# Weights into spaces that stand idle: three gate/up blocks of the last group, and one down block of two groups

## The chip, the cores and the metric

The kernel runs on one core of a Trainium2 chip. The metric is the time of one execution on the device in microseconds (us). A profile of one execution stands beside it, whose span is the time from the first to the last instruction of the program.

The engines are TensorE (PE, matmuls), VectorE (DVE), ScalarE (ACT), GpSimd (POOL) and SyncE (SP). In this kernel SP and POOL mostly ask for transfers between HBM and the on-chip memory: SP for the inputs, the gate/up weights, the outputs and the transposes, POOL for the down weights and for the attention values. Each of them issues its requests in program order, and a request that has to wait (for a buffer to be free, or for data) holds up all that is behind it.

## What is computed

A transformer block over 2048 rows of 576 numbers, in bfloat16, conditioned by a vector `c` (a shift, a scale and a gate for each of its two halves):

```python
mod = (silu(c) @ w_mod).reshape(c.shape[0], 6, 1, -1)
sa, ca, ga, sb, cb, gb = ...
h = layernorm(x) * (1 + ca) + sa
x = x + ga * attention(h)          # 32 heads of 18, each row sees 8 rows: itself and -2, -4, ... -14
h = layernorm(x) * (1 + cb) + sb
g = h @ w_gate                     # 576 x 4608
u = h @ w_up                       # 576 x 4608
x = x + gb * ((g * u) @ w_down)    # 4608 x 576
```

## The kernel before

The rows are cut into 8 chunks of 256, and the chunks into 5 groups: [0], [1, 2], [3, 4], [5, 6], [7]. For each group a gate/up phase makes hh = g * u, transposed (4608 rows as 36 f-tiles of 128), and a down phase multiplies hh by w_down and adds up over the f-tiles. All five groups read all weights again from HBM. While TensorE works on one group, attention and layernorm of the next chunks run beside it on VectorE, ScalarE and in gaps that a planner (`timed`, `among`) leaves for TensorE's share of them. The planner knows costs of the engines' work; requests for weights have no cost in it, they are put at fixed f-tiles.

**Blocks.** Weights come in blocks of 4 f-tiles, so a phase has 9 blocks (`NBLK`), numbered in the code from 0 to 8. A gate/up block is 1 MB, asked for by `load_wgu` (line 154, two requests on SP, gate and up, of 512 KB each). A down block is 576 KB, asked for by `load_wd` (line 171, one request on POOL). A block number g counts over groups, g = group x 9 + block, and numbers over 8 reach into the next group.

**Buffers.** Gate/up blocks rotate through 3 buffers (`wgup`), down blocks through 3 others (`wdp`). A block can instead be given a home of its own: `wgu_home` and `wd_home` hold a space for a block number, and the loader takes it if there is one. Before the change, the homes are these: the product space `prod_t` (the products of queries and keys, 5120 columns) takes down blocks 3 and 4 in groups 1 to 3 (5 and 6 in group 0); in groups 0 and 4, which have one chunk only, the second half of the hh tile is spare and takes some blocks, in group 4 the down blocks 3 to 6 (`ld_spare`), which wait for the landing of the last gate/up block.

**Gate/up** (`gate_up`, matmuls at line 694 in `half`). For each f-tile, gate and up matmuls run as a pair on two halves of the array. At every fourth f-tile, a block two ahead is asked for: at f = 4 block 3, at f = 8 block 4, and so on to block 8 at f = 24 (group 0 has a list of its own). A buffer is free for it when the block three before it has been read out.

**Down** (`down`, lines 895 and 900, `acc` and the narrow rest `accr`). Blocks 0 to 2 are there at the start, blocks 3 and 4 in the product space. Block 5, 6 and 7 are asked for after blocks 0, 1 and 2, block 8 after block 5, and then the first three of the next group after blocks 6 and 7 and at the end of the phase. In the middle, three gate/up blocks of the next group are asked for (f = 1, 15 and 25). The last group has a down phase of its own, `down_last` (lines 948 and 951).

**Value buffers.** Attention reads shifted copies of the values, 4608 columns per 128 rows, from two buffers in turn (`vshp`, tile `vsh`, requests at line 440 on POOL, arithmetic at lines 499 to 509, the last of which writes `o_sb`). `o_sb` is then transposed by a request on SP (line 582, to `oT`), and TensorE multiplies it by the output weights (`b_w`, lines 588 and 590) at a place that the planner sets in the down phase. After that come a layernorm, another transpose on SP (line 620, to `h2T`) and the scale and shift, before the group's gate/up can begin.

Of the kernel before, what the change touches and what calls it, by code (L numbers as in the profile page):

```python
# [7 lines left out]
BF = mybir.dt.bfloat16  # L8
# [10 lines left out]
P = 128  # L19
D = 576  # L20
# [3 lines left out]
H = 32  # L24
DH = 18
W = 8
# [9 lines left out]
NB = 512  # L36
FB = 4
# [7 lines left out]
def kernel(  # L45
# [20 lines left out]
    def pool(name, bufs, **kw):  # L66
        return ctx.enter_context(tc.tile_pool(name=name, bufs=bufs, **kw))
# [14 lines left out]
    vshp = pool("vshp", 2)  # L82
# [33 lines left out]
    prod_t = consts.tile([P, 4 * KT * CH], BF, name="prod_t")  # L116
# [25 lines left out]
    wgu_blk, wgu_in, wd_blk, wd_home, wgu_home = {}, {}, {}, {}, {}  # L142
    NG = len(GROUPS)
    NBLK = FT // FB

    def load_wgu(g):
        if g >= NG * NBLK:
            return
        cs = slice((g % NBLK) * NB, (g % NBLK + 1) * NB)
        wb = wgu_home.pop(g, None)  # L150
        if wb is None:
            wb = wgup.tile([P, KF, 2, NB], BF, name="wgu")
        for t, wsrc in enumerate((B_w_gate, B_w_up)):
            r = nc.sync.dma_start(wb[:, :, t, :], wsrc[0:KF * P, cs].rearrange("(k p) n -> p k n", p=P))
        wgu_blk[g] = wb
        wgu_in[g] = r
# [6 lines left out]
    def load_wd(g):  # L163
        if g >= NG * NBLK:
            return
        r0 = (g % NBLK) * FB * P
        wb = wd_home.pop(g, None)
        if wb is None:
            wb = wdp.tile([P, FB, D], BF, name="wd")
        wd_blk[g] = wb  # L170
        return nc.gpsimd.dma_start(wb[:], B_w_down[r0:r0 + FB * P, :].rearrange("(k p) n -> p k n", p=P))  # L171
# [624 lines left out]
    def timed(items, extra, threads, slack, busy=0.0):  # L796

        t, dve = 0.0, busy
        done, seq = {f"v{i}": 0.0 for g in GROUPS for i in g[1:]}, []
        done["late"] = 0.0  # L800
        extra, threads = list(extra), [list(th) for th in threads]

        def ready(need):
            return all(done.get(x, 1e9) <= t for x in need.split())

        def fill():
            nonlocal t, dve
            moved = True
            while moved:
                moved = False  # L810
                for th in threads:
                    if th and ready(th[0][2]) and (not th[0][1] or dve <= t + slack):
                        pe, d, _, mark, wait, call = th.pop(0)
                        t += pe
                        dve = max(dve, t) + d if d else dve
                        done[mark] = (dve if d else t) + wait
                        seq.append(("piece", call))
                        moved = True
                        break
        for kind, f, step, own, need in items:  # L820
            if seq and extra and ready(extra[0][1]):
                pe, _, mark, make = extra.pop(0)
                seq.append(("pair", make))
                t += pe
                done[mark] = t + pe + 1.0
                fill()
            assert ready(need), (need, t)
            seq.append((kind, f))
            fill()
            dve = max(dve, t) + own  # L830
            t += step
        assert not extra, (extra[0][1], t)
        return seq, [(*p[0:2], p[2] if all(x in names(th) for x in p[2].split()) else "late", *p[3:]) for th in threads for p in th]
# [22 lines left out]
    def gate_up(gi, hh, bg):  # L856
        n = len(GROUPS[gi])
        first = 2.6 if gi == 0 else 2.0 * len(GROUPS[gi - 1])
        seq, late = timed(gate_items(gi), *bg, 0.9 * n, first)
        prev = after = None  # L860
        for kind, x in seq:
            if kind == "piece":
                x()
                continue
            if after:
                after()
            cur = x() if kind == "pair" else wg_pair(gi, hh, x, kind)
            cur.first()
            after = prev.second() if prev else None
            if kind in ("f", "f1"):  # L870
                f = x
                if f > 0 and f % FB == 0:
                    ask = {1: 4, 2: 5, 3: 6, 5: 7, 6: 8}.get(f // FB, NBLK) if gi == 0 else f // FB + 2
                    if ask < NBLK:
                        load_wgu(gi * NBLK + ask)
                loads.get((gi, f), nop)()
            prev = cur
        if after:
            after()
        after = prev.second()  # L880
        if after:
            after()
        return late

    def down(gi, hh, bg):
        grp = GROUPS[gi]
        nj = ST * len(grp)
        last = FT - FB
        at, late = among(last, 0.25 * nj, bg)
        acc = [ps([P, 512], F32, "acc") for _ in range(nj)]  # L890
        accr = ps([P, 2 * ST, 64], F32, "accr")

        def mm_a(f, j):
            wb = wd_blk[gi * NBLK + f // FB]
            nc.tensor.matmul(acc[j][:], lhsT=hh[:, f, js(j)], rhs=wb[:, f % FB, 0:512],  # L895
                             start=(f == 0), stop=(f == FT - 1))

        def mm_r(f, j):
            wb = wd_blk[gi * NBLK + f // FB]
            nc.tensor.matmul(accr[:, j, :], lhsT=hh[:, f, js(j)], rhs=wb[:, f % FB, 512:D],  # L900
                             start=(f == 0 and j == 0), stop=(f == FT - 1), skip_group_check=True)

        for f in range(last):
            for j in range(nj):
                mm_a(f, j)
                mm_r(f, j)
            if f % FB == FB - 1:
                ask = {0: 7, 1: 8, 2: 9, 7: 10} if gi == 0 else {0: 5, 1: 6, 2: 7, 5: 8, 6: 9, 7: 10}
                if f // FB in ask:
                    load_wd(gi * NBLK + ask[f // FB])  # L910
            asks = (1, 5 * FB, 6 * FB + 2) if gi == 0 else (1, 4 * FB - 1, 6 * FB + 1)
            if f in asks:
                load_wgu((gi + 1) * NBLK + asks.index(f))
            for piece in at[f]:
                piece()
        xs = [t for i in grp for t in x1.pop(i)]
        for j in range(nj):
            for f in range(last, FT):
                mm_r(f, j)
        o_ts = [outp.tile([P, D], BF, name="o_t") for _ in range(nj)]  # L920
        t_r = outr.tile([P, 2 * ST, 64], BF, name="t_r")
        nc.vector.tensor_tensor(t_r[:, 0:nj, :], accr[:, 0:nj, :],
                                gb_bc[:, None, 512:D].to_broadcast([P, nj, 64]), ALU.mult)
        for j in range(nj):
            for f in range(last, FT):
                mm_a(f, j)
            nc.vector.tensor_tensor(o_ts[j][:, 0:512], acc[j][:], gb_bc[:, 0:512], ALU.mult)
        for j in range(nj):
            r0 = (grp[0] * ST + j) * P
            nc.vector.tensor_tensor(o_ts[j][:, 0:512], o_ts[j][:, 0:512], xs[j][:, 0:512], ALU.add)  # L930
            nc.vector.tensor_tensor(o_ts[j][:, 512:D], t_r[:, j, :], xs[j][:, 512:D], ALU.add)
            nc.sync.dma_start(out_flat[r0:r0 + P, :], o_ts[j][:])
        load_wd(gi * NBLK + NBLK + 2)
        return late

    def down_last(gi, hh):
# [55 lines left out]
    def behind(dma, load):  # L992
        tc.add_manual_dep(dma.ins, load.ins.name, SYNC, reason="order of the loads")
# [197 lines left out]
    def ld_spare(k):  # L1191
        g = (NG - 1) * NBLK + 3 + k
        wd_home[g] = spare[NG - 1][:, k * FB * D:(k + 1) * FB * D].rearrange("p (k d) -> p k d", d=D)
        behind(load_wd(g), wgu_in[NG * NBLK - 1])

    def ld_prods(gi):
        for k in range(2):
            g = gi * NBLK + (5 if gi == 0 else 3) + k
            wd_home[g] = prod_t[:, k * FB * D:(k + 1) * FB * D].rearrange("p (k d) -> p k d", d=D)
            load_wd(g)  # L1200

    loads = {(0, 20): lambda: behind(load_wd(1), wgu_in[6]), (0, 21): lambda: ld_d1(4), (0, 22): lambda: load_wd(2), **{(gi, 32): lambda gi=gi: ld_prods(gi) for gi in (1, 2, 3)}, (NG - 1, 28): lambda: [ld_spare(k) for k in range(4)]}

    def ld_d1(k):
        c0 = 8 * NB + FB * D if k == 3 else 0
        wd_home[k] = spare[0][:, c0:c0 + FB * D].rearrange("p (k d) -> p k d", d=D)
        load_wd(k)
# [56 lines left out]
    for gi, grp in enumerate(GROUPS):  # L1264
        hh_t = hhp.tile([P, FT * 2 * CH], BF, name="hh")
        n = CH * len(grp)
# [45 lines left out]
```

## Time and profile before

| | us |
|---|---|
| three runs | 548.65, 550.29, 550.65 |
| median | 550.29 |
| the profiled execution | 549.95 |
| its span | 548.2 |

Times in the profile are from the start of its span. Group 1's down phase runs from about 212 to 252 us, group 2's gate/up from there to 332 and its down phase to 373, group 3's gate/up to 451 and its down phase to 489, the last group's gate/up to 527 and its down phase to 543. The views used below are the page itself (a summary), the waits (who waited for whom, how long in total, how often, the longest), the timeline (instructions of an engine in order of time: start, duration, engine, line, operation, tiles written and read; behind it, in brackets, the idle time before it and what ended it), the windows (for a stretch: the mean, busy time and number of instructions of TensorE, its weight loads, VectorE, ScalarE and GpSimd, the granted clock, the DMA share and GB/s), and the view of one line, with the time from request to landing. In the queues of SP and POOL a row is the time of issuing, not of moving the data. "x2" behind a row means that two rows are shown as one.

### The profile page before, as it was taken

To read this page: it belongs to the slowest core of one execution; us is meant where nothing else is said; L and a number is where in the kernel's file an instruction comes from. 1 tells how busy PE (TensorE), PEld (TensorE's weight loads), DVE (VectorE), ACT (ScalarE), POOL (GpSimd) and SP (SyncE) were. 2 spreads that over 40 slices of the span, in tenths; PEclk is the share of its full clock that TensorE was granted. 3 is DMA by queue.
4 is the path that set the end of the run, shared out by engine and by line. 5 is a ranking of instruction groups with operands and counts; after the bars stand their busy time and mean duration, and the time that the engine had idled before them with its cause. 6 is when DMAs were issued, how large, how long until landed. Compare 5 with 4: busy or idle time off the path is not lost.

```text
span 548.2 us, 14589 instructions
## 1 busy us (share of the span) xinstructions
PE 538.7 (98%) x6190; PEld 322.5 (59%) x6190; DVE 317.6 (58%) x717; ACT 250.0 (46%) x615; POOL 70.2 (13%) x106
## 2 busy tenths in 40 slices
PE   8999999999999999999999999999999999999997
PEld 4777799756745444555544444555544445568875
DVE  5989687767866787546358896524343924031212
ACT  3666777643656564022646552103555550016630
POOL 8112111222000110112000200110020001110030
PEclk9999999999999999999999999999999999999999
DMA  8999989868873692867645972965299432758771
GB/s 285 302 299 355 306 202 315 298 183 254 299 206 88 192 287 75 206 202 236 235 110 158 260 254 69 195 205 152 92 256 291 129 90 84 228 158 273 245 234 50
DMA packets 94746, 114.52 MB, mean 209 GB/s; under 512 B 27930, under 2 KB 83370, under 8 KB 94554
## 3 DMA queue, kind: packets, MB, share of 16 engines
q1 hardware_dynamic: 83184, 67.29, 43.6%
q0 software_dynamic: 11344, 46.25, 26.8%
q8 instruction: 48, 0.79, 0.6%
q14 instruction: 16, 0.13, 0.1%
q10 hardware_dynamic: 154, 0.07, 0.0%
HBM read 103.15 MB, written 4.74 MB: 197 GB/s over the span
## 4 chain that ended last, share of the span: by engine, by line
PE 83%; DMA 7%; DVE 4%; issue 4%; ACT 1%; SPq 0%; POOL 0%; POOLq 0%; DVEq 0%; ACTq 0%
PE pg L694 25%; PE pu L694 20%; PE acc L895 16%; DMA wgu<-in_B_w_up_dram 5%; PE pq L694 3%; PE pq L401 3%; PE acc L948 3%; PE pw L590 2%; PE accr L900 2%; PE lgT L455 2%; PE pv L694 2%; DMA wd<-in_B_w_down_dram 1%; PE pv L424 1%; DVE prod_t L1033 1%; PE busy L190 1%
## 5 line engine op out<-in xcount | busy, mean ns | idle before, releaser
L694 PE MATMUL pg<-h2T,wgu 64*128 64x512 bf16 (+1 forms) x1472 | 277.7, 327 | 0.0
L694 PE MATMUL pu<-h2T,wgu 64*128 64x512 bf16 (+1 forms) x1472 | 274.1, 327 | 1.7 <-DMA wgu<-in_B_w_up_dram 1.6
L694 PEld LDWEIGHTS <-wgu 64*128 64x128 bf16 x2944 | 147.3, 94 | 98.4 <-DMA wgu<-in_B_w_up_dram 2.8
L745 ACT CAST u_sb<-pu 128x512 bf16<-128x512 f32 (+1 forms) x172 | 85.6, 497 | 142.6 <-PE pg L694 125.9
L748 DVE TENSOR_TENSOR hh<-g_sb,u_sb 128x512 bf16<-128x512 bf16 x136 | 57.4, 423 | 117.6 <-ACT g_sb L746 117.1
L895 PE MATMUL acc<-wd,hh 128*128 128x512 bf16 x376 | 93.2, 380 | 0.0
L746 ACT CAST g_sb<-pg 128x512 bf16<-128x512 f32 (+1 forms) x172 | 86.6, 504 | 0.0
L895 PEld LDWEIGHTS <-hh 128*128 128x128 bf16 x504 | 49.0, 98 | 59.6 <-issue 1.5
L900 PE MATMUL accr<-wd,hh 128*128 128x64 bf16 x376 | 63.5, 193 | 0.4 <-DMA wd<-in_B_w_down_dram 0.4
L694 PE MATMUL pu<-h2T,wgr 64*128 64x512 bf16 (+1 forms) x188 | 61.5, 327 | 0.2 <-ACT u_sb L745 0.2
L694 PE MATMUL pg<-h2T,wgr 64*128 64x512 bf16 (+1 forms) x188 | 61.5, 327 | 0.0
L171 POOL DMA_DIRECT2D wd<-in_B_w_down_dram x31 | 23.3, 751 | 227.9 <-PE pwr L588 95.6
L900 PEld LDWEIGHTS <-hh 128*128 128x128 bf16 x504 | 45.9, 98 | 2.4 <-issue 0.5
L446 DVE TENSOR_TENSOR prod_t<-qT,kT 128x1280 bf16<-128x1280 bf16 x56 | 43.7, 818 | 0.7 <-ACT kT L765 0.7
L499 DVE TENSOR_TENSOR vsh<-vsh,attn 128x1152 bf16<-128x1152 bf16 x56 | 39.6, 749 | 0.0
L694 PEld LDWEIGHTS <-wgr 64*128 64x128 bf16 x376 | 21.1, 94 | 15.4 <-issue 2.5
L895 PE MATMUL acc<-prod_t,hh 128*128 128x512 bf16 x112 | 28.9, 380 | 0.0
L440 POOL DMA_DIRECT2D vsh<-vd x14 | 12.5, 897 | 105.7 <-DVE o_sb L509 79.2
L296 ACT ACTIVATE h2T<-h2T,modc 128x256 bf16<-128x256 bf16 x12 | 6.6, 594 | 37.6 <-DMA h2T<-xn 37.6
L401 PE MATMUL pq<-hT,wqk 128*128 128x256 bf16 (+1 forms) x225 | 21.8, 251 | 0.5 <-DVE hT L294 0.5
L694 PE MATMUL pq<-hT,wqk 64*128 64x256 bf16 (+1 forms) x360 | 21.7, 259 | 0.0
L900 PE MATMUL accr<-prod_t,hh 128*128 128x64 bf16 x112 | 21.6, 193 | 0.0
(201 smaller groups left out, 565.5 us busy)
## 6 DMA issues: line engine op xcount, KB each, us to landing
wgu<-in_B_w_gate_dram SPq DMA_DIRECT2D x44, 512.0 KB, 4.6
wgu<-in_B_w_up_dram SPq DMA_DIRECT2D x44, 512.0 KB, 7.7
wd<-in_B_w_down_dram POOLq DMA_DIRECT2D x31, 576.0 KB, 4.9
vsh<-vd POOLq DMA_DIRECT2D x14, 1152.0 KB, 9.5
prod_t<-in_B_w_down_dram POOLq DMA_DIRECT2D x8, 576.0 KB, 10.3
hh<-in_B_w_down_dram POOLq DMA_DIRECT2D x6, 576.0 KB, 8.1
x_r<-in_A_x_dram SPq DMA_DIRECT2D x8, 288.0 KB, 11.8
vd<-v_sb POOLq DMA_DIRECT2D x16, 144.0 KB, 5.0
```

The costliest lines, as they stand in the source:

```text
L171: return nc.gpsimd.dma_start(wb[:], B_w_down[r0:r0 + FB * P, :].rearrange("(k p) n -> p k n", p=P))
L401: nc.tensor.matmul(pq[:, gi, :], lhsT=wqk[:, kt, m * P:(m + 1) * P], rhs=hT[:, kt, cols], start=(kt == 0), stop=(kt == KT - 1))
L440: return nc.gpsimd.dma_start(vsh[:].rearrange("p w d h -> p w (d h)"), vsrc)
L446: nc.vector.tensor_tensor(prod, aa[i]["qT"][:], aa[i]["kT"][:, :, off:off + CH], ALU.mult)
L499: nc.vector.tensor_tensor(v, v, at, ALU.mult)
L694: return nc.tensor.matmul(out, lhsT=lhs, rhs=rhs, start=first, stop=last, skip_group_check=True)
L745: nc.scalar.copy(u[:, c, :], pu)
L746: nc.scalar.copy(g[:, c, :], pg)
L748: return lambda: nc.vector.tensor_tensor(hh[:, f - c:f + 1, :], g, u, ALU.mult)
L895: nc.tensor.matmul(acc[j][:], lhsT=hh[:, f, js(j)], rhs=wb[:, f % FB, 0:512], start=(f == 0), stop=(f == FT - 1))
L900: nc.tensor.matmul(accr[:, j, :], lhsT=hh[:, f, js(j)], rhs=wb[:, f % FB, 512:D], start=(f == 0 and j == 0), stop=(f == FT - 1), skip_grou ...
L948: nc.tensor.matmul(acc[i][:], lhsT=hh[:, f, js(j)], rhs=wb(f)[:, c0:c1], start=(f == 0), stop=(f == FT - 1))
```

## The change

- In group 4 the gate/up blocks 3 and 4 (the fourth and fifth) get the two value buffers, and block 8 (the ninth) the product space. Blocks 3 and 4 are asked for in the gate/up of group 3, at f = 34. In group 4's gate/up the remaining four blocks, 5 to 8, are asked for at f = 4, 8, 12 and 16.
- In groups 1 and 2 the down block 8 gets a value buffer and is asked for together with block 6, after block 1. The first three down blocks of the next group, numbers 9 to 11, are asked for one step earlier each (after blocks 5, 6 and 7), and the request at the end of the phase goes.
- Groups 0 and 3 ask for their down blocks as before; their lists are only written in another form.

```diff
-                    ask = {1: 4, 2: 5, 3: 6, 5: 7, 6: 8}.get(f // FB, NBLK) if gi == 0 else f // FB + 2
+                    ask = {0: {1: 4, 2: 5, 3: 6, 5: 7, 6: 8}, NG - 1: {1: 5, 2: 6, 3: 7, 4: 8}}.get(gi, {k: k + 2 for k in range(NBLK)}).get(f // FB, NBLK)
                     if ask < NBLK:
                         load_wgu(gi * NBLK + ask)
                 loads.get((gi, f), nop)()
...
+    def value_space():
+        return vshp.tile([P, W, DH, H], BF, name="vsh").rearrange("p w d h -> p (w d h)")
+
+    def wgu_spaces():
+        for k, space in ((3, value_space()), (4, value_space()), (8, prod_t)):
+            wgu_home[(NG - 1) * NBLK + k] = space[:, 0:8 * NB].rearrange("p (k t n) -> p k t n", t=2, n=NB)
+        load_wgu((NG - 1) * NBLK + 3)
+        load_wgu((NG - 1) * NBLK + 4)
+
+    WD_ASKS = [{0: (7,), 1: (8,), 2: (9,), 7: (10,)},
+               {0: (5,), 1: (6, 8), 2: (7,), 5: (9,), 6: (10,), 7: (11,)},
+               {0: (5,), 1: (6, 8), 2: (7,), 5: (9,), 6: (10,), 7: (11,)},
+               {0: (5,), 1: (6,), 2: (7,), 5: (8,), 6: (9,), 7: (10,)}]
...
-                ask = {0: 7, 1: 8, 2: 9, 7: 10} if gi == 0 else {0: 5, 1: 6, 2: 7, 5: 8, 6: 9, 7: 10}
-                if f // FB in ask:
-                    load_wd(gi * NBLK + ask[f // FB])
+                if gi in (1, 2) and f // FB == 1:
+                    wd_home[gi * NBLK + 8] = value_space()[:, 0:FB * D].rearrange("p (k d) -> p k d", d=D)
+                for k in WD_ASKS[gi].get(f // FB, ()):
+                    load_wd(gi * NBLK + k)
...
-        load_wd(gi * NBLK + NBLK + 2)
+        if gi in (0, 3):
+            load_wd(gi * NBLK + NBLK + 2)
...
-    loads = {(0, 20): lambda: behind(load_wd(1), wgu_in[6]), (0, 21): lambda: ld_d1(4), (0, 22): lambda: load_wd(2), **{(gi, 32): lambda gi=gi: ld_prods(gi) for gi in (1, 2, 3)}, (NG - 1, 28): lambda: [ld_spare(k) for k in range(4)]}
+    loads = {(0, 20): lambda: behind(load_wd(1), wgu_in[6]), (0, 21): lambda: ld_d1(4), (0, 22): lambda: load_wd(2), **{(gi, 32): lambda gi=gi: ld_prods(gi) for gi in (1, 2, 3)}, (3, 34): wgu_spaces, (NG - 1, 28): lambda: [ld_spare(k) for k in range(4)]}
```

## The prediction

> **What bounds the kernel now.** First the page: its span and its line of busy times.
>
> ```profile
> span 548.2 us, 14589 instructions
> PE 538.7 (98%) x6190; PEld 322.5 (59%) x6190; DVE 317.6 (58%) x717; ACT 250.0 (46%) x615; POOL 70.2 (13%) x106
> ```
>
> TensorE is busy for 538.7 of 548.2 us, so only idle TensorE time and the start and end of the span can be won without taking matmuls away, and the change takes none away. So the next view is the list of TensorE's waits, cut to 100 to 545 us, which leaves the start-up out. Its columns are the total, the number of waits and the longest.
>
> ```profile
> engine line waited for: us in total, times, longest us
> PE pu L694 <- DMA wgu<-in_B_w_up_dram: 1.6, 2, 0.8
> PE accr L900 <- DMA wd<-in_B_w_down_dram: 0.4, 1, 0.4
> ```
>
> That is the whole list: three waits, all for weights. The timeline of TensorE shows where they are and what they really take, because the ends of matmuls are modelled and a wait is only counted from such an end. I read start to start.
>
> ```profile
> 323.53 0.38 PE L694 MATMUL pg<-h2T,wgu 64*128 64x512 bf16 x1
> 324.04 0.39 PE L694 MATMUL pu<-h2T,wgu 64*128 64x512 bf16 x1
> ...
> 368.80 0.19 PE L900 MATMUL accr<-wd,hh 128*128 128x64 bf16 x1
> 369.39 0.39 PE L900 MATMUL accr<-wd,hh 128*128 128x64 bf16 x8 [0.40 <-DMA wd<-in_B_w_down_dram]
> ...
> 490.01 0.27 PE L694 MATMUL pg<-h2T,wgr 64*128 64x256 bf16 x1
> 500.81 0.27 PE L694 MATMUL pg<-h2T,wgr 64*128 64x256 bf16 x1
> 500.92 0.27 PE L694 MATMUL pg<-h2T,wgu 64*128 64x256 bf16 x1
> 501.93 0.28 PE L694 MATMUL pu<-h2T,wgu 64*128 64x256 bf16 x1 [0.74 <-DMA wgu<-in_B_w_up_dram]
> ...
> 513.63 0.27 PE L694 MATMUL pg<-h2T,wgu 64*128 64x256 bf16 x1
> 514.74 0.28 PE L694 MATMUL pu<-h2T,wgu 64*128 64x256 bf16 x1 [0.84 <-DMA wgu<-in_B_w_up_dram]
> ```
>
> In the last group's gate/up the gate and up matmuls run as a pair and start together, so the pair at 500.92 stands for 501.93 - 500.92 = 1.01 us and the one at 513.63 for 514.74 - 513.63 = 1.11 us. The down phase of group 2 loses 369.39 - 368.80 = 0.59 us where eight such small matmuls need 0.39 us, one step of about 0.03 us: 0.56 us. A fourth gap, 0.51 us at 323.53 in group 2's gate/up, is too short to be listed as a wait; the change does not touch what feeds it.
>
> Why these three? The queue of SP shows the requests of the last gate/up.
>
> ```profile
> 494.16 0.39 SPq L154 DMA_DIRECT2D wgu<-in_B_w_gate_dram  x1
> 494.60 0.50 SPq L154 DMA_DIRECT2D wgu<-in_B_w_up_dram  x1
> 498.09 0.37 SPq L154 DMA_DIRECT2D wgu<-in_B_w_gate_dram  x1
> ...
> 506.94 0.37 SPq L154 DMA_DIRECT2D wgu<-in_B_w_gate_dram  x1
> 507.36 0.50 SPq L154 DMA_DIRECT2D wgu<-in_B_w_up_dram  x1
> ...
> DMA to landing us min/median/max: 3.9/5.4/7.3
> ```
>
> The last line is the landing time of these requests from the view of line 154 between 489 and 520 us. With three buffers, block 3 (counted from 0) is asked for only when block 0 is read out, at 494.16 us, and is needed at 500.92: 6.8 us ahead, while its up half is issued at 494.60 and lands 7.3 us later. The same for block 6: 506.94, and needed at 513.63. One f-tile takes (500.81 - 490.01) / 11 = 0.98 us here, a block of four 3.93 us, in which 1 MB must come. So it is the lead, not TensorE, that is short by about 1 us.
>
> **The change part by part.** (1) Blocks 3 and 4 of the last gate/up get the two value buffers, asked for in group 3. Are they free? The last reads of the buffers, in the timeline of VectorE, and of the product space, which block 8 takes, in TensorE's:
>
> ```profile
> 211.55 0.46 DVE L509 TENSOR_TENSOR o_sb<-vsh 128x576 bf16<-128x576 bf16 x1
> ...
> 329.94 0.46 DVE L509 TENSOR_TENSOR o_sb<-vsh 128x576 bf16<-128x576 bf16 x1
> ...
> 438.77 0.46 DVE L509 TENSOR_TENSOR o_sb<-vsh 128x576 bf16<-128x576 bf16 x1
> ...
> 473.64 0.19 PE L900 MATMUL accr<-prod_t,hh 128*128 128x64 bf16 x1
> ```
>
> They are free at 439.2 us. SP is in order: behind the transposes of the last attention output it issues blocks 3 and 4, and only then block 0, which it issues at 440.57 now.
>
> ```profile
> 440.57 0.52 SPq L154 DMA_DIRECT2D wgu<-in_B_w_gate_dram  x1
> ...
> 463.56 2.53 SPq L620 DMA_TRANSPOSE h2T<-xn  x2
> ...
> 440.00:450.00 10.00, 10.00 (x96) 4.48 (x92) 2.13 (x5) 5.64 (x11) 0.00 (x0) 1.00 0.44 121
> 450.00:460.00 10.00, 10.00 (x85) 4.94 (x82) 3.61 (x9) 2.05 (x4) 0.75 (x1) 1.00 0.21 61
> 500.00:510.00 10.00, 9.26 (x169) 8.02 (x167) 2.12 (x5) 6.03 (x19) 0.00 (x0) 1.00 0.81 251
> ```
>
> The last two columns of the windows are the DMA share and GB/s. Four more issues of about 0.5 us put block 0 at some 442.7 us; it is needed just before 490.01. The added 2.1 MB at the 251 GB/s of the last row take 8.4 us, and the DMA engines are idle for 5.6 + 7.9 = 13.5 us of those 20. SP's next work, the transposes, comes at 463.56. So the move costs nothing; without that empty stretch it would be up to 8.4 us of delay on SP's transfers.
>
> (2) In the last gate/up four blocks are asked for instead of six. Block 5 goes out when block 0 is read out, at 494.2, and is needed at f = 20, which without the stalls is 500.81 + 8 x 0.98 = 508.7 us: a lead of 14.5 us in place of 6.8. Blocks 6 and 7 follow at 498.1 and about 502.0 with the same lead; block 8 has its own space, free since 473.6, and goes out right behind block 7, needed at 520.4. 4.2 MB at 251 GB/s are 16.7 us, so the last lands near 511, ahead of its need by 9. Both stalls go: -1.01 - 1.11 = -2.12 us. The four down blocks in the spare half of hh wait for the last gate/up block, so they now start near 511 and come in before the down phase begins; TensorE waits for none of them before, so this is worth nothing.
>
> (3) The ninth down block (8) in groups 1 and 2. POOL's queue around group 2's down:
>
> ```profile
> 222.78 0.75 POOL L171 DMA_DIRECT2D wd<-in_B_w_down_dram  x1 [5.62 <-PE accr L900]
> ...
> 343.87 0.75 POOL L171 DMA_DIRECT2D wd<-in_B_w_down_dram  x1 [6.17 <-PE accr L900]
> 347.25 0.75 POOL L171 DMA_DIRECT2D wd<-in_B_w_down_dram  x1 [2.63 <-PE accr L900]
> 361.45 0.75 POOL L171 DMA_DIRECT2D wd<-in_B_w_down_dram  x1 [13.45 <-PE accr L900]
> ```
>
> Block 8 leaves at 361.45 and is used at about 368.8; now it leaves behind block 6, at 344.6, into a value buffer that has been free since 329.9 (in group 1 at 223.5, free since 211.6). No wait is added in front of block 7 at 347.25. That is -0.56 us in group 2, nothing in group 1, where TensorE did not wait. The next group's three down blocks each move one request earlier, which only empties the queue sooner. Its two value loads: one buffer is now read by TensorE until the end of the down phase, but they stood behind a request that waited for the same matmuls, so they lose nothing.
>
> The instructions are the same in number and kind on every engine; all that moves are requests. **Sum:** -2.12 - 0.56 = -2.68 us. The profiled execution took 549.95 us, so 547.27. It lies 0.34 us under the median of the three runs, 550.29; from that median the sum gives **547.6 us**, or -0.49%. What a measurement of this kernel can tell from no change is about 0.5%, 2.75 us, so the forecast falls just inside it. By the idle times as listed (0.74 + 0.84 + 0.40 = 1.98) it would be 548.3; I take start to start, since a late pair delays all behind it by its whole lateness.
>
> **The rivals.** *(A) The wait moves instead of going.* Landing times are not fixed. Here is a request that lands late, from SP's timeline, and the landing line of line 154 over the whole run:
>
> ```profile
> 310.63 0.82 SPq L154 DMA_DIRECT2D wgu<-in_B_w_up_dram  x1
> ...
> DMA to landing us min/median/max: 3.7/5.6/16.3
> ```
>
> If one of blocks 5 to 8 took 16.3 us, against a lead of 14.5, 1.8 us of the 2.68 would come back: 549.5. Against it, the longest in that stretch was 7.3. *(B) More is won:* the 0.51 us at 323.53 goes as well, since the value loads of group 2's start leave earlier: 547.1. The block that is late there left at 310.63, long after, so I expect no such thing.
>
> *(C) Slower.* In groups 1 and 2 the ninth block's 576 KB now run on POOL's queue while SP's queue has transposes, and TensorE, in order, multiplies by one of these, oT, soon after:
>
> ```profile
> 217.37 3.40 SPq L582 DMA_TRANSPOSE oT<-o_sb  x2
> ...
> 337.91 3.41 SPq L582 DMA_TRANSPOSE oT<-o_sb  x2
> ...
> DMA to landing us min/median/max: 2.6/3.4/4.2
> ...
> 228.20 0.31 PE L588 MATMUL pwr<-wo,oT 128*128 128x64 bf16 x5
> ```
>
> The landing line is that of group 1's transposes of oT; the row above it is group 2's pair, issued by 341.3, before block 6. Counted from the end of the issue, 220.77, with the longest landing of 4.2, group 1's is there by 225.0, 3.2 us before its use at 228.20. A stall begins when the extra block holds a transpose back by more than these 3.2 us, and the kernel is slower than before when the two phases together lose more than 2.68, that is at a delay above 4.5 us. At 6.0 us in each it would lose 2 x (6.0 - 3.2) = 5.6, less 2.68: 553.2. Against it: these transposes are issued over 3 us ahead of the extra request, and 0.59 MB at 251 GB/s are 2.3 us. The Trainium skill, DMA: Bandwidth & Descriptors, section Queues, rings and completion order, speaks for it: each DMA engine takes turns between the queues at the boundary of a packet, so a small transpose packet would wait behind a large weight packet, whatever queue it came by. No run here shows yet how long that is at this place.
>
> *(D) It doesn't do what it says:* a request sits in SP's queue behind a buffer that is not free, and the lead stays as it was: 550.3.
>
> **How the numbers follow.** Forecast (all three stalls go) 0.72, A 0.09, B 0.10, C 0.04, D 0.05. Faster by over 0.5% means below 547.54. The forecast of 547.6 sits on that edge, and the runs of before spread over 2 us, so its 0.72 is cut in halves, 0.36 and 0.36; B adds 0.10: faster 0.46. Same: 0.36 + A 0.09 + D 0.05 = 0.50. Slower: C, 0.04. The range reaches up to A at 549.5 and down to 546.3, which is B less 0.8 for the spread of a median; outside it lie C, D and some of the tails.
>
> **What would show it.** TensorE's waits after 100 us list nothing for wgu in the last gate/up, and the gap at the end of group 2's down is gone; the pairs run at 0.98 us per f-tile from the first to the last; SP issues three gate/up blocks near 440 us and four between 494 and 504. The span falls by 2.7 us, 2.1 of it after 489 us. It is wrong if a wait for wgu stands at f = 20 to 32 (A), if line 588 waits for oT in groups 1 or 2 (C), or if the stalls go and the end does not move with them.

## The result, and the profile after

The changed kernel takes 547.75 us (median of 9 runs, 547.21 to 548.31) where the kernel before, run beside it, takes 549.83 (9 runs, 548.41 to 550.84). The ratio is 0.9964, with a 95% interval of 0.9951 to 0.9977 (here and below it is worked out over the runs of both kernels and need not be that of the two medians): faster by 0.36%, a difference that the interval tells from none, but under the 0.5% that the prediction drew as its line. The forecast was 547.6. The profiled executions are 549.95 before and 547.78 after.

The page of the changed kernel, its span and busy times:

```profile
span 546.1 us, 14594 instructions
PE 537.9 (99%) x6190; PEld 324.7 (59%) x6190; DVE 318.1 (58%) x717; ACT 249.9 (46%) x615; POOL 70.2 (13%) x106
```

TensorE does the same 6190 matmuls in a span 2.1 us shorter. Its waits from 100 to 545 us (total, number, longest):

```profile
engine line waited for: us in total, times, longest us
PE pu L694 <- DMA wgu<-in_B_w_up_dram: 0.3, 1, 0.3
```

None of the three waits for weights is left at its place. Where block 3 of the last gate/up begins, the gate and up matmuls again start together, now reading `vsh`, and the narrow matmuls at the end of group 2's down run on without a gap (17 of them from 368.95 to 369.61):

```profile
368.95 0.19 PE L914 MATMUL accr<-wd,hh 128*128 128x64 bf16 x1
368.98 0.63 PE L914 MATMUL accr<-vsh,hh 128*128 128x64 bf16 x16
...
500.78 0.27 PE L694 MATMUL pg<-h2T,vsh 64*128 64x256 bf16 x1
500.78 0.27 PE L694 MATMUL pu<-h2T,vsh 64*128 64x256 bf16 x1
```

The one wait in the list is the fourth gap of the prediction, grown long enough to be listed. TensorE's timeline there:

```profile
323.52 0.38 PE L694 MATMUL pg<-h2T,wgu 64*128 64x512 bf16 x1
324.19 0.39 PE L694 MATMUL pu<-h2T,wgu 64*128 64x512 bf16 x1 [0.29 <-DMA wgu<-in_B_w_up_dram]
```

Start to start it is 324.19 - 323.52 = 0.67 us where it was 0.51. The windows show what the requests became (the last two columns are the DMA share and GB/s):

```profile
440.00:450.00 10.00, 10.00 (x96) 5.31 (x94) 2.41 (x6) 5.37 (x10) 0.00 (x0) 1.00 0.96 287
450.00:460.00 10.00, 10.00 (x84) 4.99 (x79) 3.43 (x9) 2.05 (x4) 0.75 (x1) 1.00 0.34 105
500.00:510.00 10.00, 10.00 (x188) 8.93 (x186) 2.13 (x5) 6.64 (x22) 0.00 (x0) 1.00 0.93 307
```

The stretch that was half empty at 440 us is now full, and from 500 to 510 the window counts 188 matmuls where it counted 169. SP's queue puts the requests where the prediction had them:

```profile
440.56 0.45 SPq L154 DMA_DIRECT2D vsh<-in_B_w_gate_dram  x1
441.80 0.37 SPq L154 DMA_DIRECT2D vsh<-in_B_w_gate_dram  x1
442.81 0.59 SPq L154 DMA_DIRECT2D wgu<-in_B_w_gate_dram  x1
...
494.02 0.39 SPq L154 DMA_DIRECT2D wgu<-in_B_w_gate_dram  x1
...
502.92 1.48 SPq L154 DMA_DIRECT2D prod_t<-in_B_w_gate_dram  x1
```

Blocks 3 and 4 go to `vsh`, block 0 follows at 442.81 (worked out: 442.7), block 5 leaves at 494.02, block 8 goes to `prod_t` at 502.92, right behind block 7. The landing line of these requests, line 154 between 489 and 521 us:

```profile
DMA to landing us min/median/max: 4.5/6.3/7.4
```

Before it was 3.9, 5.4 and 7.3. So the blocks do not land faster than before; they are asked for earlier, and a landing of 7.4 us lies well inside a lead of 14.5.

How much of the gain lies in the last group? VectorE's timeline has a fixed mark at each end: `t_r`, at the end of group 3's down, and the last `o_t` of the kernel. Before:

```profile
486.10 0.42 DVE L922 TENSOR_TENSOR t_r<-accr,gb_bc 128x256 bf16<-128x256 f32 x1 [17.23 <-PE accr L900]
...
545.36 0.29 DVE L969 TENSOR_TENSOR o_t<-o_t,x 128x256 bf16<-128x256 bf16 x1
```

And after:

```profile
485.96 0.42 DVE L937 TENSOR_TENSOR t_r<-accr,gb_bc 128x256 bf16<-128x256 f32 x1 [17.08 <-PE accr L914]
...
543.18 0.29 DVE L985 TENSOR_TENSOR o_t<-o_t,x 128x256 bf16<-128x256 bf16 x1
```

From mark to mark the last group takes 59.26 us before and 57.22 after: 2.04 us less. All that comes earlier is worth only 486.10 - 485.96 = 0.14 us.

### The profile page after: what moved, and what is told of

It is laid out like the page before. It is cut to its first block, busy times and chain, and to the rows that moved or that the text cites. A ratio compares the mean times of both kernels' runs of the same rounds, so it can differ in the third digit from the quotient of the medians.

```text
span 546.1 us, 14594 instructions
## 1 busy us (share of the span) xinstructions
PE 537.9 (99%) x6190; PEld 324.7 (59%) x6190; DVE 318.1 (58%) x717; ACT 249.9 (46%) x615; POOL 70.2 (13%) x106
## 4 chain that ended last, share of the span: by engine, by line
PE 91%; DVE 4%; DMA 2%; ACT 1%; issue 0%; SPq 0%; DVEq 0%; ACTq 0%
PE pg L694 26%; PE pu L694 22%; PE acc L909 20%; PE pq L694 3%; PE pw L590 3%; PE pq L401 3%; PE accr L914 3%; PE acc L964 3%; DMA wgu<-in_B_w_up_dram 2%; PE lgT L455 2%; PE pv L694 2%; PE pv L424 1%; DVE prod_t L1049 1%; PE busy L190 1%; PE po L552 1%; PE pwj L569 0%
## 5 line engine op out<-in xcount | busy, mean ns | idle before, releaser
L694 PE MATMUL pg<-h2T,wgu 64*128 64x512 bf16 (+1 forms) x1376 | 266.4, 332 | 0.0
L694 PE MATMUL pu<-h2T,wgu 64*128 64x512 bf16 (+1 forms) x1376 | 261.0, 332 | 0.3 <-DMA wgu<-in_B_w_up_dram 0.3
L694 PEld LDWEIGHTS <-wgu 64*128 64x128 bf16 x2752 | 138.8, 94 | 93.7 <-DMA wgu<-in_B_w_up_dram 1.1
L909 PE MATMUL acc<-wd,hh 128*128 128x512 bf16 x344 | 86.0, 380 | 0.0
L914 PE MATMUL accr<-wd,hh 128*128 128x64 bf16 x344 | 62.4, 193 | 0.0
L171 POOL DMA_DIRECT2D wd<-in_B_w_down_dram x29 | 21.8, 751 | 228.5 <-PE pwr L588 96.1
```

Of the source, the lines that this page charges most:

```text
L694: return nc.tensor.matmul(out, lhsT=lhs, rhs=rhs, start=first, stop=last, skip_group_check=True)
```

## The experiments

Two theories stood against each other. **Theory:** each wait is a weight block that lands later than its lead allows, its lateness is paid once, and each part of the change pays back its own gaps. **Rival:** the waits are one matter of the load on the DMA engines; taking one away moves it or changes the others. Four kernels ran on one chip at a time beside the kernel before, in three sets, so times are compared within a set. Each kernel also left one profile, of one execution. The diffs show long lines in part; what stands behind `#` was put in for the reader.

**First set** (kernel before: 549.07 us, median of 26 runs, 547.88 to 551.34).

The changed kernel once more, no edit. 

> The changed kernel once more, on the chip of its parts. If the gain is the three waits that went (1.01 + 1.11 + 0.56 us), less what other places gave back in the profiled pair (0.15 in group 2's gate/up, 0.3 in group 3's gate/up), it is 2.0 to 2.7 us under the kernel before, about 547.5. If the first comparison was luck of the runs, it lies within 1 us of the kernel before.

547.49 us (547.36 to 548.03), ratio 0.9965 (0.9951 to 0.9979). The gain is there again, 1.6 us by the medians, though less than the 2.0 to 2.7 expected: the waits had been priced from one execution.

The last group's part alone:

```diff
-               {0: (5,), 1: (6, 8), 2: (7,), 5: (9,), 6: (10,), 7: (11,)},   # groups 1 and 2
+               {0: (5,), 1: (6,), 2: (7,), 5: (8,), 6: (9,), 7: (10,)},
...
-                if gi in (1, 2) and f // FB == 1:
-                    wd_home[gi * NBLK + 8] = value_space()[:, 0:FB * D].rearrange("p (k d) -> p k d", d=D)
...
-        if gi in (0, 3):
-            load_wd(gi * NBLK + NBLK + 2)
+        load_wd(gi * NBLK + NBLK + 2)
```

> Only the last group's gate/up blocks get their spaces; the ninth down block stays as it was. Theory (each wait is worth its start-to-start lateness): 2.1 us under the kernel before, with the gap of about 0.6 us at the end of group 2's down still there. Rival (the two parts share one cause, the load on the queues): the gap in group 2's down changes too, or the gain differs from 2.1 by more than 0.5 us.

548.55 us (548.14 to 552.59), ratio 0.9999 (0.9983 to 1.0016). By the time, the expectation of 2.1 us is missed: 0.5 us by the medians. By the trace the last group does what was expected: from mark to mark it takes 57.23 us, as in the changed kernel. Against the first profile of the kernel before, this execution lost 0.6 us before 50 us and 0.3 us at 323.5, where the gap is 0.84; the gap at the end of group 2's down is there as before, 0.53 us (370.31 - 369.75, less one step of 0.03). This kernel touches none of these places. One profile can't say what the other runs of this set lost, so the next set repeats this kernel.

The ninth down block alone:

```diff
-  ask = {0: {1: 4, 2: 5, 3: 6, 5: 7, 6: 8}, NG - 1: {1: 5, 2: 6, 3: 7, 4: 8}}.get(gi, {k: k + 2 for k in range(NBLK)}).get(f // FB, NBLK)
+  ask = {1: 4, 2: 5, 3: 6, 5: 7, 6: 8}.get(f // FB, NBLK) if gi == 0 else f // FB + 2
...
-  (3, 34): wgu_spaces,
```

> Only the ninth down block of groups 1 and 2 moves. Theory: the gap at the end of group 2's down goes (0.56 us), both gaps of the last gate/up stay at 1.0 and 1.1, so 0.3 to 0.6 us under the kernel before, which the time alone can hardly tell. Rival (the ninth block holds back transposes): TensorE waits at the output projection in group 1 or 2, and the time is that of the kernel before or more.

549.06 us (547.32 to 551.31), ratio 1.0004 (0.9990 to 1.0019): nothing that the time can tell. In its trace the gap of group 2's down is gone and no output projection waits; the two gaps of the last gate/up are there, but as 0.51 and 0.83 us, not 1.01 and 1.11. That speaks for gaps that differ from execution to execution, which the next set tests.

The gap that the change leaves:

```diff
-            load_wd(g)                    # ld_prods: down blocks 3 and 4, to the product space
+            r = load_wd(g)
+            if gi > 0:
+                behind(r, wgu_in[gi * NBLK + NBLK - 1])
```

> The changed kernel, and the two down blocks for the product space in groups 1 to 3 wait for the landing of their group's last gate/up block. Theory of the gap that is left at 323.5 us (0.66 us): the late gate/up block shares the DMA engines with 1.18 MB of these down blocks and gets only some 60 to 80 KB per us beside them; with them behind it, it lands some 4 us earlier, the gap goes, and the kernel is 0.5 to 0.9 us under the changed kernel. Rival (the block is late because SP issues it late, 310.05 us, behind the transposes): the gap stays above 0.4 us and the time is that of the changed kernel.

546.81 us (5 runs, 546.80 to 547.34), ratio 0.9960 (0.9947 to 0.9973): 0.68 us under the changed kernel on the same chip, as much as the gap was there (0.67). SP still issues the block at the same place, 310.06, and POOL now asks for the product space at 321.09 instead of 309.90, still 25 us before its first use at 346.3. The landing line of line 154 between 302 and 320 us, of the changed kernel and of this one:

```profile
DMA to landing us min/median/max: 8.9/11.1/13.5
```

```profile
DMA to landing us min/median/max: 6.1/9.4/9.9
```

The longest landing falls by 3.6 us, and TensorE's timeline runs through the place without a gap:

```profile
323.32 0.38 PE L694 MATMUL pu<-h2T,wgr 64*128 64x512 bf16 x1
323.54 0.38 PE L694 MATMUL pg<-h2T,wgu 64*128 64x512 bf16 x1
323.54 0.38 PE L694 MATMUL pu<-h2T,wgu 64*128 64x512 bf16 x1
```

So the late issue behind SP's transposes does not by itself make this block late; without the 1.18 MB beside it on the other queue it is in time. The DMA packets of the changed kernel show how the two queues share: first from 318 to 320 us, with POOL's queue (q0) and SP's (q1) both at work, then from 322 to 324, with SP's alone. The columns are the queue, its packets, MB, and the time of its packets as a share of the engines' time (packets that overlap can bring it over 100%).

```profile
q0 software_dynamic: 146, 0.60, 80.3%
q1 hardware_dynamic: 150, 0.15, 22.9%
...
q1 hardware_dynamic: 699, 0.70, 109.6%
```

Side by side the two queues move almost the same number of packets, but POOL's are some four times as large, so SP's weights get 0.15 MB in 2 us where they get 0.70 alone.

**Second set** (kernel before: 549.10 us, 29 runs, 547.62 to 552.88).

The kernel before, no edit. 

> The kernel before once more, for a second profile of it. If the three waits are the same in every execution, the gaps are again near 0.5, 0.6, 1.0 and 1.1 us. If they come and go with the load on the DMA engines, as the second kernel with the unchanged last group suggests (0.51 and 0.83 us there), they differ by some tenths.

The four gaps are now 0.49, 0.47, 0.86 and none: in the last gate/up only block 3 is late, block 6 is in time. They come and go, as expected. Its marks around the last group:

```profile
487.64 0.42 DVE L922 TENSOR_TENSOR t_r<-accr,gb_bc 128x256 bf16<-128x256 f32 x1 [16.96 <-PE accr L900]
...
545.74 0.29 DVE L969 TENSOR_TENSOR o_t<-o_t,x 128x256 bf16<-128x256 bf16 x1
```

That is 58.10 us, 1.16 us less than in the first profile of the same kernel.

The last group's part alone, again, no new edit. 

> The last group's part alone, a second time. In its first run its trace gained 2.0 us in the last group, as worked out, and lost 0.6 us between 39 and 50 us, where nothing is changed, and 0.3 us at the gap that stays in group 2's gate/up. If that start-up loss was chance, it isn't in the second profile and the time comes to 0.8 to 2 us under the kernel before; if the change of the order of requests brings it, it is there again.

547.80 us (547.38 to 549.03), ratio 0.9978 (0.9960 to 0.9996): 1.3 us under the kernel before by the medians, inside what was expected. Its last group again takes 57.23 us. The loss between 39 and 50 us is not there; this execution lost 1.7 us near 9 us instead, in a wait for the first big weight. The gaps at 323.5 and at the end of group 2's down are too short to be listed as waits, but they are there:

```profile
325.27 0.38 PE L694 MATMUL pg<-h2T,wgu 64*128 64x512 bf16 x1
325.48 0.39 PE L694 MATMUL pu<-h2T,wgu 64*128 64x512 bf16 x1
...
370.25 0.92 PE L914 MATMUL accr<-wd,hh 128*128 128x64 bf16 x17
```

The first is 0.21 us. The second is 0.26: these 17 matmuls take 0.92 us where they took 0.66 in the changed kernel.

Only blocks 3 and 4 get spaces, block 8 rotates:

```diff
-  NG - 1: {1: 5, 2: 6, 3: 7, 4: 8}
+  NG - 1: {1: 5, 2: 6, 3: 7, 5: 8}
...
-        for k, space in ((3, value_space()), (4, value_space()), (8, prod_t)):
+        for k, space in ((3, value_space()), (4, value_space())):
```

> As the changed kernel, but block 8 of the last gate/up has no space of its own: it takes the buffer of block 5, so it is asked for at f = 24 and needed at f = 32, a lead of about 6.8 us in place of 17. Theory (a lead of 6.8 us is short by the landing time): one gap is back, near 519 us, of 0.4 to 1.0 us, and the kernel is slower than the changed one by as much. Rival (the DMA engines' load, not the lead, made the waits; the load is now less, since block 8 is the last and alone): no gap, and the time of the changed kernel.

547.45 us (546.93 to 549.54), ratio 0.9974 (0.9954 to 0.9994). The theory's gap did not come: the last group takes 57.22 us. Block 8's requests, in the view of line 154 between 513 and 516 us:

```profile
DMA to landing us min/median/max: 3.7/3.7/3.7
```

With nothing queued before it, the block lands in 3.7 us, well inside its lead. My expectation was wrong, and it need not have been: in the kernel before, blocks 5 and 8 have that same short lead and wait for nothing. (Blocks 4 and 7 have about 1 us more there: the stall ahead of them puts off their use, not their request.) A short lead is a risk, not a wait. The one wait of this execution is the gap at 323.5, which is 1.43 us long here.

The ninth down block sooner:

```diff
-               {0: (5,), 1: (6, 8), 2: (7,), 5: (9,), 6: (10,), 7: (11,)},   # groups 1 and 2
+               {0: (5, 8), 1: (6,), 2: (7,), 5: (9,), 6: (10,), 7: (11,)},
...
-                if gi in (1, 2) and f // FB == 1:
+                if gi in (1, 2) and f // FB == 0:
```

> As the changed kernel, but the ninth down block is asked for after block 0, right behind block 5 and in the middle of SP's transposes of oT, some 6 us earlier. Theory: the transposes have 3 us of slack and the block takes 2 to 4 us of the engines, so TensorE's wait at the output projection is 0 to 0.5 us and the time that of the changed kernel. Rival C of the prediction (packets of a large transfer hold back the small ones of a transpose): the transposes land more than 3 us later, line 588 waits for oT by 1 us or more in each of the two groups.

547.39 us (547.02 to 550.21), ratio 0.9977 (0.9959 to 0.9996). The landing line of group 1's transposes of oT (line 582, 215 to 222 us), in the changed kernel and with the block beside them:

```profile
DMA to landing us min/median/max: 2.8/3.6/4.4
```

```profile
DMA to landing us min/median/max: 4.7/5.5/6.3
```

The use of oT in TensorE's timeline of the latter:

```profile
228.22 0.31 PE L588 MATMUL pwr<-wo,oT 128*128 128x64 bf16 x5
```

The block holds the transposes back by 1.9 us, and TensorE uses oT at 228.22 as ever (228.20 before). The delay that rival C speaks of is real; even where it is provoked it stays inside the slack. The gap at 323.5 is 0.28 us here, below what the list of waits shows.

**Third set** (kernel before: 548.97 us, 29 runs, 547.49 to 552.91).

The changed kernel a third time, no edit. 

> The changed kernel on the chip of the three next ones, as their measure. 1.5 to 2.2 us under the kernel before, as twice already; in its profile no gap in the last gate/up and none at the end of group 2's down, and a gap at 323.5 us that may be anything from 0 to 1.4.

547.34 us (547.20 to 556.09, one run far above the other nine, which end at 547.74), ratio 0.9959 (0.9938 to 0.9979). Gap at 323.5: 0.48 us; none in the last gate/up.

The product-space blocks behind, again, no new edit. 

> The changed kernel with the product-space blocks behind the last gate/up block, a second time, now to tell it from the changed kernel on the same chip. Theory: 0.4 to 0.9 us under the changed kernel, and no gap at 323.5 us again. Rival: the gap was absent by chance, as in one execution with the ninth block asked for sooner; then the gap is there or the two kernels' times agree within 0.2 us.

546.86 us (546.81 to 548.15), ratio 0.9955 (0.9936 to 0.9973), 0.48 us under the changed kernel, and again no gap. The two kernels' middle halves don't overlap in either set.

One space only:

```diff
-  NG - 1: {1: 5, 2: 6, 3: 7, 4: 8}
+  NG - 1: {1: 4, 2: 5, 3: 6, 5: 7, 6: 8}
...
-        for k, space in ((3, value_space()), (4, value_space()), (8, prod_t)):
+        for k, space in ((3, value_space()),):
...
-        load_wgu((NG - 1) * NBLK + 4)
```

> As the changed kernel, but of the last gate/up only block 3 gets a space; blocks 4 to 8 rotate (asked for at f = 4, 8, 12, 20, 24). Leads to the up half: 10 us for blocks 4 to 6, 6.3 us for blocks 7 and 8. Theory (the wait is a landing of 4 to 7.3 us against a lead of 6.3, long only when other transfers or a neighbour block stand before it): no gap for blocks 4 to 6, and at blocks 7 and 8 none or one under 0.9 us; time 0 to 0.9 us over the changed kernel. Rival (every block with a lead of 6.3 us waits): two gaps, at f = 28 and 32, 1.5 to 2 us over the changed kernel.

547.72 us (547.05 to 549.72), ratio 0.9975 (0.9958 to 0.9991), 0.4 us over the changed kernel by the medians. Its marks around the last group, and the landing line of its blocks 7 and 8 (line 154 from 512 us):

```profile
487.92 0.42 DVE L936 TENSOR_TENSOR t_r<-accr,gb_bc 128x256 bf16<-128x256 f32 x1 [17.07 <-PE accr L913]
...
545.14 0.29 DVE L984 TENSOR_TENSOR o_t<-o_t,x 128x256 bf16<-128x256 bf16 x1
```

```profile
DMA to landing us min/median/max: 3.8/3.9/3.9
```

57.22 us: one space already gives the whole gain of the last group in this execution, though by the medians this kernel is slower than the changed one. The profile is nevertheless of an execution of 549.72 us, and its waits in the first 14 us say why:

```profile
PE pm L318 <- DMA wmA<-in_w_mod_dram: 2.4, 1, 2.4
```

TensorE waits 2.4 us for the first big weight of the kernel. The kernel before waits there for nothing in its first profile and for 1.3 us in its second. No kernel here touches that place; 2.4 us are 0.4% of the time, as much as the change is worth.

The product-space blocks behind, on the kernel before:

```diff
-            load_wd(g)                    # in ld_prods of the kernel before
+            r = load_wd(g)
+            if gi > 0:
+                behind(r, wgu_in[gi * NBLK + NBLK - 1])
```

> The kernel before with nothing but the product-space blocks behind the last gate/up block. Theory: the gap at 323.5 us goes and the other three stay, so 0.3 to 0.9 us under the kernel before. Rival: the late blocks are all one matter of the load on the DMA engines, so that the gaps of the last group shrink as well: over 1.3 us under the kernel before.

548.25 us (546.84 to 550.03), ratio 0.9978 (0.9962 to 0.9994), 0.7 us under the kernel before. The gap at 323.5 is gone, the other three stay:

```profile
501.48 0.28 PE L694 MATMUL pu<-h2T,wgu 64*128 64x256 bf16 x1 [0.95 <-DMA wgu<-in_B_w_up_dram]
```

Block 3 is late by 1.22 us (501.48 - 500.26), block 6 by 0.61, the ninth block by 0.41. So the waits are separate, each with its own relief, and the rival of one common load falls.

**All traces together.** The last group from mark to mark takes 59.26, 58.10, 58.52 and 58.97 us in the four profiles with the old requests (the kernel before twice, the ninth block alone, the product-space blocks alone), and 57.22 or 57.23 us in all ten with at least one space. The gap at 323.5 is in all eleven profiles where the product-space blocks are not held back (0.21 to 1.43 us), and in none of the three where they are. The gap at the end of group 2's down is in all five profiles with the ninth block's old request (0.26 to 0.56 us, 0.45 on the mean), and in none of the nine with the new one.

## Why the prediction was right, point by point

**The bound.** That only idle TensorE time could be won held: the matmuls are the same, and the span fell with the waits.

**Blocks 3 and 4, block 8, the four requests (-2.12 us).** The two gaps went, and from mark to mark the last group lost 2.04 us in the profiled pair. The mechanism held in every trace: the landings stayed as long as they were (up to 7.4 us) and the leads grew. One line was read too closely: the landing of 7.3 us that the prediction gives to block 3 is block 6's (507.36 to 514.69), and block 3's up half has no landing on record; TensorE starts on it 7.33 us after its request (501.93 - 494.60), so the argument is the same. The size was that of one execution, and a bad one: over the four profiles with the old requests the loss against 57.22 is 2.04, 0.88, 1.30 and 1.75, on the mean 1.49 us. That is the term that was mis-sized: the median should lose about 1.5 us there, not the 2.1 of this one execution. The extra traffic near 440 us cost nothing; block 0 left at 442.8 and the transposes at 463 were not disturbed.

**The ninth down block (-0.56 us).** Its gap is gone in every trace with the part, and 0.56 us too is more than the mean of 0.45. In the profiled pair the gain was eaten: of the 0.56, 0.15 went to the gap at 323.5, which grew to 0.67, and some 0.3 to small steps where no wait is listed, 0.08 near 424 us and 0.19 near 454; only 0.14 was left at the mark at 486. The gap at 323.5 grows and shrinks in any kernel (0.21 to 1.43), so its part is chance. The small steps are chance as well: in the changed kernel's next profile they are not there, and its mark comes 0.40 us before that of the kernel before, the 0.56 less the 0.16 of the gap at 323.5:

```profile
485.70 0.42 DVE L937 TENSOR_TENSOR t_r<-accr,gb_bc 128x256 bf16<-128x256 f32 x1 [16.92 <-PE accr L914]
```

By its time alone the part can't be told from nothing.

**The sum.** -2.68 in the profiled pair was -2.17 (549.95 to 547.78). Three comparisons of medians gave 2.1, 1.6 and 1.6 us; the two terms at their means, 1.49 and 0.45, would have been 1.94. That the forecast of 547.6 came within 0.2 us is luck: the sum was too large, and the prediction took it from the higher of its two bases, 550.29. A later median of the same kernel, 549.07, would have given 546.4, with 547.49 measured on that chip. The choice between start to start and the listed idle times (1.98) is settled by the marks: in the four profiles with the old requests the last group is longer by 2.04, 0.88, 1.30 and 1.75 us, its gaps start to start are 2.12, 0.86, 1.34 and 1.83, and the listed idle times come to 1.58 in the first.

**The chances.** "Within 0.5%" was the likeliest, 0.50 against 0.46, and 0.9964 lies there.

**The rivals.** A, a late landing, did not occur: TensorE waited for no block of the last gate/up in any trace with at least one space. (By the prediction's own sum A would have been 549.4, not 549.5.) B, that the gap at 323.5 goes as well, did not come by itself, and the reason given against it was right: it needed another cure. C's delay was provoked and measured: 1.9 us, inside the slack. The slack was also larger than the prediction worked out. A landing is counted from the start of its request, and the prediction added the longest one to the end of both issues. Group 1's two transposes start at 217.37 and 219.58 and land 4.2 and 2.6 us later, at 221.6 and 222.2, so the slack before 228.20 is 6.0 us, not 3.2. The Trainium skill's rule (DMA: Bandwidth & Descriptors, section Queues, rings and completion order) is that each DMA engine takes turns between queues at packet boundaries. The trace agrees in that two busy queues move nearly equal numbers of packets (146 and 150 from 318 to 320 us) whatever their size; whether what the profile counts as a packet is the page's packet or a part of it, no run here shows. D fell with SP's queue: the requests left at the times worked out.

**What was missed.** The spread. The kernel before ranges over 2.4 to 5.4 us in its sets, and the profiles show two sources: the wait at the start (0 to 2.4 us) and the gaps that come and go. A range from one profile and three runs held the result, but the waits of one bad execution were taken for their usual size.

## What to carry to other kernels

A wait seen in one profile is a draw: before it is priced, take a second execution, or the lead and the landing times that make it, and use the middle. A block with a lead of 6.3 us and landings between 3.7 and 7.3 waits sometimes. Giving one block a longer lead can also empty the queue in front of the next ones (with one space, blocks 7 and 8 landed in 3.8 to 3.9 us), so try the smallest move first: in its one profile one space did for the last group what three do, though by the medians that kernel was 0.4 us slower. And when a late transfer was issued late, ask also what it shares the engines with: holding back two transfers by 11 us, 25 us ahead of their use, was worth 0.5 to 0.7 us more.

## What the runs showed that I had not expected

- A request of one size (512 KB of gate/up weights on SP's queue) lands in 3.7 us alone and in 13.5 us near 310 us beside others; holding back the 1.18 MB beside it took 3.6 us off. Two busy queues share the DMA engines by packets, not by bytes: the one with 1 KB packets got a fifth of the bytes.
- The first big weight of the kernel (`wmA`) keeps TensorE waiting for 0 to 2.4 us, from execution to execution.
- The fastest kernel here is the changed one with the product-space blocks held back: 546.81 and 546.86 us against 547.49 and 547.34 for the changed kernel and 549.07 and 548.97 for the kernel before on the same chips.
